# Retention attention into a snake feed-forward: the last nine chunks loaded head by head and worked in four 64x64 tiles

## The chip, the cores and the metric

The kernel runs on one core of a Trainium2 chip. The core has a matrix engine (TensorE: PE for its matmuls, PEld for its weight loads), three elementwise engines (VectorE = DVE, ScalarE = ACT, GpSimd = POOL) and SyncE (SP), which here only issues transfers. The transfers run on 16 DMA engines that all queues share. The metric is the device time of one execution in microseconds (us), as a median of several runs. A profile is one further execution that the hardware recorded; its span is the time from the first to the last instruction.

## What is computed

```python
# q, k, v: (4, 8, 768, 64) float32; gamma[h] = 1 - 2**(-5 - h), scale = 1/8
for t in range(S):
    state = gamma * state + k[:, :, t] (outer) v[:, :, t]
    y[:, :, t] = scale * q[:, :, t] @ state
x = y.transpose(0, 2, 1, 3).reshape(3072, 512)
h = x @ w_in                        # (512, 2048)
g = h + sin(alpha * h)**2 / (alpha + 1e-9)
out = g @ w_out                     # (2048, 512) -> (3072, 512) float32
```

## The kernel before

**Tiling.** Each of the 4 batches is cut into 6 chunks of 128 tokens, so there are 24 chunks. A chunk is worked for its 8 heads together. `P` is the order in which the chunks are worked: `P[0..3]` are the first chunks of the four batches (`e0` to `e3`), then come chunks 1 to 5 of batch 0 (`P[4..8]`), of batch 1 (`P[9..13]`), of batch 2 (`P[14..18]`) and of batch 3 (`P[19..23]`). The nine chunks that the change touches are `P[15..18]` and `P[19..23]`.

**Attention of a chunk.** `turn` (L202) has the DMA engines transpose q and k of the chunk into `qkT`, issued on SP. `stage_A` (L207) makes the scores of all 8 heads with 8 matmuls (L213), each with 64 rows and 128 columns of the array, and VectorE multiplies them by a causal mask into `aT` (L217). `stage_M` (L236) adds two products in `py`: the state times q (8 matmuls, L247) and `aT` times v (8 matmuls, L251), both in 128 rows and 64 columns. VectorE takes `py` out times the q decay into `xT` (L258). `stage_S` (L220, 8 matmuls, L227) adds k times v to the state `ps`, which stays in PSUM for a batch, and `keep_S` (L231) copies it to the block-diagonal `s_bd` on ScalarE. The decay of v is multiplied into v beforehand by `scale_v` (L111), from `P[6]` on on GpSimd.

**Feed-forward.** The chunks are taken in seven groups of 4, 2, 4, 4, 4, 4 and 2 chunks (`sizes`, L49). `phase` (L392) does the first product of a group in 16 slots (8 for the two groups of two): a `Slot` is 4 matmuls with `w_in` (L279), Sin and Square on ScalarE, and one combining instruction on VectorE (L294). In the same slot stand matmuls with `w_out` of the group before (`ff_out`, L304). So the PE always has a slot of 4 + 4 matmuls of 128x512. I write (g, n) for slot n of group g.

**Where attention stands.** The attention of a group's chunks is set into the slots of the group before: `where` (L538) puts `P[11..14]` at slots 5, 8, 11 and 14 of group 2, `P[15..18]` at slots 2, 6, 10 and 14 of group 3, `P[19..22]` at the same slots of group 4, and `P[23]` at (5,6). At `where[n]` stand, in this order, the scores of `P[n]`, the rest of `P[n-1]`, and the transpose of `P[n+2]` (L552 to L560). Everything on an engine runs in the order in which the program writes it (`manual_schedule`).

**Loads.** All chunk loads are issued by GpSimd, q, k and v of a chunk each in one transfer that also turns float32 to bf16 (`load_chunk`, L73; L83). GpSimd's program alternates three loads and a decay of v (L504 to L517); a load also waits in the program for the load eight before it, whose semaphore it takes over. The list runs down to `P[23]`, and the decays of `e2` and `e3` stand behind the loads of `P[13]` and `P[15]`.

Of the kernel before, what the change touches and what calls it, by code (L numbers as in the profile page):

```python
# [8 lines left out]
F32 = mybir.dt.float32  # L9
BF16 = mybir.dt.bfloat16  # L10
ACTF = mybir.ActivationFunctionType
ALU = mybir.AluOpType
# [3 lines left out]
def kernel(  # L16
# [15 lines left out]
    nc = tc.nc  # L32
    B, H, S, D = q.shape
    C = 128
    NCH = S // C
    NJ = B * NCH
    NP = H // 2
    d_model = H * D
    d_ff = moe_w_in.shape[1]
    KS = d_model // 128  # L40
# [8 lines left out]
    sizes = [4, 2, 4, 4, 4, 4, 2]  # L49
# [3 lines left out]
    place = {j: (g, i) for g, js in enumerate(groups) for i, j in enumerate(js)}  # L53

    consts = ctx.enter_context(tc.tile_pool(name="consts", bufs=1))
    big = ctx.enter_context(tc.tile_pool(name="big", bufs=1))
    work = ctx.enter_context(tc.tile_pool(name="work", bufs=2))
    psum = ctx.enter_context(tc.tile_pool(name="psum", bufs=1, space=bass.MemoryType.PSUM))
# [8 lines left out]
    raw = {}  # L67

    def chunk_of(t, j):
        b, c = divmod(j, NCH)  # L70
        return t[b, :, c * C:(c + 1) * C, :].rearrange("h s d -> s h d")

    def load_chunk(j, names="qkv"):  # L73
        for name, src in (("q", q), ("k", k), ("v", v)):
            if name not in names:
                continue
            if name == "v":
                t = big.tile([128, H, D], BF16, name="vr", tag="vr", bufs=NJ)
            else:
                if ("qk", j) not in raw:  # L80
                    raw["qk", j] = big.tile([128, 2, H, D], BF16, name="qkr", tag="qkr", bufs=NJ)
                t = raw["qk", j][:, "qk".index(name)]
            nc.gpsimd.dma_start(out=t, in_=chunk_of(src, j))  # L83
            raw[name, j] = t

    WP = 4
    fw = d_ff // WP
# [8 lines left out]

    near = {}
    for name, src in (("q", q), ("k", k)):
        near[name] = big.tile([128, H, D], F32, name=f"{name}0")
        nc.sync.dma_start(out=near[name], in_=chunk_of(src, 0))  # L100
        raw[name, 0] = big.tile([128, H, D], BF16, name=f"{name}b")
    alpha_row = consts.tile([FF, 128], F32, name="alpha_row")
# [2 lines left out]
    tio = consts.tile([128, C], F32, name="tio")  # L105
    nc.gpsimd.iota(tio, pattern=[[1, C]], channel_multiplier=0, base=0, allow_small_or_imprecise_dtypes=True)
    pos = consts.tile([128, NCH], F32, name="pos")
# [1 line left out]


    def scale_v(j, eng):  # L111
        eng.tensor_mul(raw["v", j], raw["v", j], kg[:, j % NCH, :, None].to_broadcast([128, H, D]))  # L112

    load_chunk(0, "v")
    load_chunk(order[1])
# [20 lines left out]
    lg = consts.tile([128, H], F32, name="lg")  # L136
# [14 lines left out]
    for p in range(NP):  # L151
        for e in range(2):
# [2 lines left out]
    expo = consts.tile([128, NCH, H], F32, name="expo")  # L155
    nc.vector.tensor_mul(expo, pos[:, :, None].to_broadcast([128, NCH, H]),
                         lg[:, None, :].to_broadcast([128, NCH, H]))
    qg = consts.tile([128, NCH, NP, C], F32, name="qg")
    kg = consts.tile([128, NCH, H], F32, name="kg")
    step = consts.tile([128, NCH, NP], F32, name="step")  # L160
# [8 lines left out]
    alpha_sb = consts.tile([128, FF], F32, name="alpha_sb")  # L169
    rec_alpha = consts.tile([128, FF], F32, name="rec_alpha")  # L170
    s_bd = [big.tile([128, NP, 128], BF16, name=f"s_bd{i}") for i in range(2)]


    st = {}
    xT = {}

    def half_T(j, i, eng):

        if i == 0:
            st["qkT", j] = work.tile([128, 2 * NP, 128], BF16, name="qkT", tag="qkT", bufs=6)  # L180
        pt = psum.tile([128, NP, 128], BF16, name="pt", tag="mm", bufs=4)
        for p in range(NP):
            nc.tensor.transpose(pt[:, p, :], raw["qk"[i], j][:, 2 * p:2 * p + 2, :].rearrange("p h d -> p (h d)"), ident)
        o = st["qkT", j][:, i * NP:(i + 1) * NP, :]
        if eng is nc.scalar:
            nc.scalar.copy(o, pt)
        else:
            nc.vector.tensor_copy(o, pt)
# [13 lines left out]
    def turn(j):  # L202

        st["qkT", j] = work.tile([128, 2 * NP, 128], BF16, name="qkT", tag="qkT", bufs=6)
        nc.sync.dma_start_transpose(out=st["qkT", j], in_=raw["qk", j].rearrange("p i h d -> p (i h d)"))

    def stage_A(j):  # L207
        qkT = st["qkT", j]
# [22 lines left out]
    def keep_S(j, ps):  # L231
        for e in range(2):
            r = slice(64 * e, 64 * e + 64)
            nc.scalar.copy(s_bd[(j % NCH + 1) % 2][r, :, r], ps[r, :, :])  # L234

    def stage_M(j):  # L236
        c = j % NCH
        g, i = place[j]
        if g not in xT:
            xT[g] = work.tile([128, KS, sizes[g] * C], BF16, name="xT", tag="xT", bufs=3)  # L240
        qkT, aT, vs = st["qkT", j], st["aT", j], raw["v", j]
        py = psum.tile([128, NP, 128], F32, name="py", tag="ty")
        if c > 0:
            for p in range(NP):
                for e in range(2):
                    r = slice(64 * e, 64 * e + 64)
                    nc.tensor.matmul(py[r, p, :], s_bd[c % 2][:, p, r], qkT[:, p, :],  # L247
                                     start=(p == 0), stop=True, skip_group_check=True)
        for p in range(NP):
            for e in range(2):  # L250
                nc.tensor.matmul(py[64 * e:64 * e + 64, p, :], vs[:, 2 * p + e, :], aT[:, e, p, :],  # L251
                                 start=(c == 0 and p == 0), stop=True, skip_group_check=True)
        x = xT[g][:, :, i * C:(i + 1) * C]
        if c == 0:
            nc.scalar.copy(x, py)
            return
        ps = stage_S(j) if c < NCH - 1 else None
        nc.vector.tensor_mul(x, py, qg[:, c])  # L258
        if ps is not None:
            keep_S(j, ps)  # L260


    gT = {}
# [72 lines left out]
    def out_pieces(g, tss):  # L336
        return [lambda ts=ts, f=f: ff_out(g, ts, f) for ts in tss for f in range(FF)]
# [5 lines left out]
    def idle_work(n):  # L343
        for _ in range(n):
            nc.tensor.matmul(spare["ps"], warm[:, :128], warm, start=True, stop=True)  # L345
# [5 lines left out]
    e0, e1, e2, e3 = order[:B]  # L351
# [4 lines left out]
    idle_work(2)  # L356
    nc.vector.tensor_mul(dec.rearrange("p e n t -> p (e n) t"), dec.rearrange("p e n t -> p (e n) t"), mask_bc)
    half_T(e0, 1, nc.scalar)
    nc.scalar.activation(out=kg, in_=expo, func=ACTF.Exp, scale=-1.0)
    for c in range(1, NCH):  # L360
        nc.scalar.activation(out=step[:, c, :], in_=lgp, func=ACTF.Exp, scale=float(C * c))
    idle_work(2)
    stage_A(e0)
    half_T(e1, 0, nc.scalar)
# [20 lines left out]
    decay_table(1)  # L385
    idle_work(5)
    stage_M(e2)
    decay_table(2)
    idle_work(3)


    def phase(g, outs, att, nf=1):  # L392

        no, done = len(outs), 0
        for n in range(FF // nf):
            now = Slot(g, n * nf, nf=nf).sq("A")
            for fn in att.get(n, ()):
                fn()
            now.add()
            while done < no * (n + 1) * nf // FF:  # L400
                outs[done]()
                done += 1
# [4 lines left out]
    def X(j):  # L407
        return lambda: turn(j)

    def A(j):  # L410
        return lambda: stage_A(j)

    def M(j):
        return lambda: stage_M(j)

    def SK(j):
        return lambda: keep_S(j, stage_S(j))
# [3 lines left out]
    P = order  # L421
    n3, n4 = 3 * C, 4 * C
    def F(ts, fs):
        for f in fs:
            for t in ts:
                ff_out(0, t, f)

    def early(f, tag="mm"):
        return Slot(0, f, (0, n3), tag=tag)

    a = early(0)
# [4 lines left out]
    b = early(1)  # L436
    a.sq("A").add()
    a = early(2)
    b.sq("A")
    c = early(3)  # L440
# [3 lines left out]
    b = early(4, "ps")  # L444
    c.sq("A")
    a.add()
    a = early(5)
# [3 lines left out]
    c = early(6)  # L451
    a.sq("A")
    b.add()
    b = early(7)
# [7 lines left out]
    F((0,), range(4))  # L462
    F((1,), range(3))
    b.add()
    a = Slot(0, 0, (n3, n4), 4)
    F((1,), (3,))
    a.sq("A").add()
    a = Slot(0, 8)
    b = Slot(0, 4, (n3, n4), 4)
    a.sq("A").add()  # L470
    a = Slot(0, 9)
    b.sq("D").add()
    F((0, 1), (4,))
    b = Slot(0, 10)
    a.sq("A").add()
    F((0, 1), (5,))
    a = Slot(0, 11)
# [3 lines left out]
    b = Slot(0, 12)  # L481
# [3 lines left out]
    a = Slot(0, 13)  # L485
    b.sq("D").add()
    F((0, 1), (9,))
    b = Slot(0, 14)
# [3 lines left out]
    a = Slot(0, 15)  # L492
# [16 lines left out]
    load_chunk(P[10])  # L509
    scale_v(P[8], nc.gpsimd)  # L510
    scale_v(e1, nc.gpsimd)
    for n in range(11, NJ + 2):
        scale_v(P[n - 2], nc.gpsimd)
        if n < NJ:
            load_chunk(P[n])
        if n in (13, 15):
            scale_v(P[(n - 9) // 2], nc.gpsimd)  # L517

    outs = out_pieces(0, (2, 3))

# [17 lines left out]
    where = {10: (2, 1)}  # L538
    for g in range(2, NG - 1):
        first = P.index(groups[g + 1][0])  # L540
# [8 lines left out]
    def at(place, fn):  # L549
        atts[place[0]].setdefault(place[1], []).append(fn)  # L550

    for n in range(10, NJ + 1):  # L552
        if n < NJ:
            at(where[n], A(P[n]))
        if n > 10:
            at(where[n], M(P[n - 1]))
        if n < NJ and P[n] % NCH == 1:
            at(where[n], SK(P[n] - 1))
        if n + 2 < NJ:
            at(where[n], X(P[n + 2]))  # L560
    for g in range(2, NG):
        phase(g, out_pieces(g - 1, range(sizes[g - 1])), atts[g], 1 if sizes[g] > 2 else 2)
    for fn in out_pieces(NG - 1, range(sizes[-1] - 1)):
# [30 lines left out]
```

## Time and profile before

| What | Value |
|---|---|
| Time of the kernel, 4 runs | median 216.48 us (216.33 to 218.24) |
| Profiled execution: its own time / its span | 216.54 us / 214.8 us |
| PE busy share; POOL, DVE, ACT | 96%; 42%, 59%, 76% |
| Mean granted TensorE clock | 1.000 |
| A decay of v on POOL (L112), x21 | 1058 ns each |
| `aT` on DVE (L217, 128x1024), x20 | 1220 ns each |
| `xT` on DVE (L258, 128x512), x20 | 682 ns each |
| Copy of the state on ACT (L234, 64x256), x40 | 360 ns each |

The profile's page gives for each group of instructions the busy time, the mean of one and the idle time of the engine before it with what ended it. A matmul's duration there includes its way through the array; what one costs in a row of many is the distance between the starts of neighbours. The "chain that ended last" is followed back from the last instruction, at each step to what released it.

### The profile page before, as it was taken

What the parts mean: (1) busy time and instruction counts of PE and PEld (TensorE: products, weight loads), DVE (VectorE), ACT (ScalarE), POOL (GpSimd) and SP (SyncE); (2) the same over time, 40 slices, a digit from 0 to 9 for tenths busy, and PEclk for the clock granted to TensorE, in tenths of its full rate; (3) what the DMA queues carried; (4) which work ended last, traced back from release to release, by engine and by line L of the source; (5) the groups of instructions that cost most, each with busy time, mean ns of one, the idle gap of its engine ahead of it and who ended that gap; (6) DMA issues with size and microseconds to landing.
All of it is one profiled execution on the core that took longest, in us unless ns stands there. A gap on an engine that the chain in (4) does not pass through costs nothing.

```text
span 214.8 us, 4304 instructions
## 1 busy us (share of the span) xinstructions
PE 206.1 (96%) x1685; PEld 108.7 (51%) x1685; DVE 127.5 (59%) x213; ACT 162.6 (76%) x311; POOL 90.0 (42%) x105
## 2 busy tenths in 40 slices
PE   7898899999999999999999999999999999999994
PEld 3444554466764545544544554554444444566554
DVE  4785669866896777774664664664644545333311
ACT  7778796658889898897787787787778877666630
POOL 8976335998669699695992300000000000000000
PEclk9999999999999999999999999999999999999999
DMA  9999999999999999999999743041011001111112
GB/s 130 149 196 187 205 207 169 154 139 240 147 150 202 147 156 153 153 159 184 130 154 143 90 101 89 9 102 50 2 49 52 32 16 49 52 49 49 52 49 98
DMA packets 100852, 24.93 MB, mean 116 GB/s; under 512 B 93392, under 2 KB 97888, under 8 KB 100832
## 3 DMA queue, kind: packets, MB, share of 16 engines
q0 software_dynamic: 77024, 13.37, 84.4%
q1 hardware_dynamic: 23808, 11.28, 26.7%
q8 instruction: 13, 0.21, 0.4%
q14 instruction: 7, 0.06, 0.1%
HBM read 27.27 MB, written 6.29 MB: 156 GB/s over the span
## 4 chain that ended last, share of the span: by engine, by line
PE 76%; DVE 10%; DMA 4%; POOL 4%; ACT 3%; issue 1%; POOLq 0%; DVEq 0%
PE po L304 35%; PE ph L279 31%; DVE gT L294 5%; DMA qkr<-in_k_dram 4%; PE py L247 3%; PE pa L213 2%; POOL qkr L83 2%; DVE aT L217 2%; PE py L251 2%; PE poh L327 2%; ACT s L282 2%; POOL vr L83 1%; ACT s L287 1%; PE ps L227 1%; DVE xT L258 1%
## 5 line engine op out<-in xcount | busy, mean ns | idle before, releaser
L294 DVE SCALAR_TENSOR_TENSOR gT<-s,rec_alpha,ph 128x512 bf16<-128x512 f32 (+3 forms) x120 | 74.1, 637 | 70.9 <-ACT s L287 70.5
L279 PE MATMUL ph<-xT,w_in 128*128 128x512 bf16 (+3 forms) x480 | 98.0, 336 | 0.8 <-DVE gT L294 0.5
L304 PE MATMUL po<-w_out,gT 128*128 128x512 bf16 x368 | 95.0, 380 | 0.6 <-DVE gT L294 0.6
L282 ACT ACTIVATE s<-ph,alpha_sb 128x512 f32<-128x512 f32 (+3 forms) x120 | 69.6, 601 | 33.1 <-PE ph L279 33.0
L279 PEld LDWEIGHTS <-w_in 128*128 128x128 bf16 x480 | 45.5, 98 | 42.3 <-issue 1.4
L287 ACT ACTIVATE s<-s 128x512 f32<-128x512 f32 (+1 forms) x94 | 58.4, 621 | 2.6
L304 PEld LDWEIGHTS <-gT 128*128 128x128 bf16 x368 | 33.9, 98 | 36.7 <-issue 0.6
L112 POOL TENSOR_TENSOR vr<-vr,kg 128x512 bf16<-128x512 bf16 x21 | 22.0, 1058 | 17.4 <-DMA vr<-in_v_dram 17.4
L217 DVE TENSOR_TENSOR aT<-pa,mask 128x1024 bf16<-128x1024 f32 x20 | 24.4, 1220 | 0.3 <-PE pa L213 0.3
L83 POOL DMA_DIRECT2D vr<-in_v_dram x24 | 21.8, 907 | 3.3 <-DMA w_in<-in_moe_w_in_dram 1.7
L83 POOL DMA_DIRECT2D qkr<-in_q_dram x23 | 21.3, 927 | 4.1 <-DMA w_out<-in_moe_w_out_dram 1.7
L83 POOL DMA_DIRECT2D qkr<-in_k_dram x23 | 20.5, 891 | 3.7 <-DMA w_out<-in_moe_w_out_dram 3.3
L234 ACT CAST s_bd<-ps 64x256 bf16<-64x256 f32 x40 | 14.4, 360 | 2.4 <-PE ps L227 2.1
L316 ACT COPY o_sb<-po 128x512 f32<-128x512 f32 x23 | 13.1, 576 | 3.9 <-PE po L304 3.9
L258 DVE TENSOR_TENSOR xT<-py,qg 128x512 bf16<-128x512 f32 x20 | 13.6, 682 | 1.1 <-PE py L251 1.1
L345 PE MATMUL spare<-warm 128*128 128x512 bf16 x28 | 9.3, 456 | 1.2 <-DVE warm L131 1.2
L213 PEld LDWEIGHTS <-qkT 64*128 64x128 bf16 x192 | 5.4, 94 | 10.0 <-issue 6.7
L213 PE MATMUL pa<-qkT 64*128 64x128 bf16 x192 | 9.5, 219 | 0.9 <-DMA qkT<-qkr 0.3
L251 PE MATMUL py<-aT,vr 128*64 128x128 bf16 x192 | 9.5, 220 | 0.4 <-DVE rec_alpha L383 0.2
L247 PE MATMUL py<-qkT,s_bd 128*64 128x128 bf16 x160 | 8.3, 225 | 0.1
L251 PEld LDWEIGHTS <-vr 128*64 128x64 bf16 x192 | 6.8, 110 | 1.3 <-issue 1.0
L247 PEld LDWEIGHTS <-s_bd 128*64 128x64 bf16 x160 | 5.2, 109 | 3.3 <-ACT s_bd L234 0.8
(61 smaller groups left out, 74.1 us busy)
## 6 DMA issues: line engine op xcount, KB each, us to landing
out_dram<-o_sb SPq DMA_DIRECT2D x23, 256.0 KB, 2.3
vr<-in_v_dram POOLq DMA_DIRECT2D x24, 128.0 KB, 6.7
qkr<-in_q_dram POOLq DMA_DIRECT2D x23, 128.0 KB, 5.8
qkr<-in_k_dram POOLq DMA_DIRECT2D x23, 128.0 KB, 5.9
w_in<-in_moe_w_in_dram POOLq DMA_DIRECT2D x4, 512.0 KB, 10.7
w_out<-in_moe_w_out_dram POOLq DMA_DIRECT2D x4, 512.0 KB, 14.6
qkT<-qkr SPq DMA_TRANSPOSE x17, 6.3
q<-in_q_dram SPq DMA_DIRECT2D x1, 256.0 KB, 3.2
```

Of the source, the lines that this page charges most:

```text
L83: nc.gpsimd.dma_start(out=t, in_=chunk_of(src, j))
L112: eng.tensor_mul(raw["v", j], raw["v", j], kg[:, j % NCH, :, None].to_broadcast([128, H, D]))
L213: nc.tensor.matmul(pa[:, e, p, :], qkT[r, NP + p, :], qkT[r, p, :], start=(p == 0), stop=True, skip_group_check=True)
L217: nc.vector.tensor_mul(aT.rearrange("p e n t -> p (e n) t"), pa.rearrange("p e n t -> p (e n) t"), m)
L247: nc.tensor.matmul(py[r, p, :], s_bd[c % 2][:, p, r], qkT[:, p, :], start=(p == 0), stop=True, skip_group_check=True)
L251: nc.tensor.matmul(py[64 * e:64 * e + 64, p, :], vs[:, 2 * p + e, :], aT[:, e, p, :], start=(c == 0 and p == 0), stop=True, skip_group_che ...
L258: nc.vector.tensor_mul(x, py, qg[:, c])
L279: nc.tensor.matmul(self.ph[:, m, :], w_in[:, i, f * 128:(f + 1) * 128], xT[g][:, i, self.lo:self.hi], start=(m == 0 and i == 0), stop=(i = ...
L282: nc.scalar.activation(out=self.s[:, m, :], in_=self.ph[:, m, :], func=ACTF.Sin, scale=alpha_sb[:, f:f + 1])
L287: nc.scalar.activation(out=self.s, in_=self.s, func=ACTF.Square)
L294: nc.vector.scalar_tensor_tensor(gT[self.g][:, f, self.lo:self.hi], self.s[:, m, :], rec_alpha[:, f:f + 1], self.ph[:, m, :], op0=ALU.mult ...
L304: nc.tensor.matmul(po[g, ts], gT[g][:, f, ts * C:(ts + 1) * C], w_out[:, f, :], start=(f == 0), stop=(f == FF - 1))
```

## The change

`wide(j)` is true for the nine chunks. They are loaded by `load_seq`, batch by batch: q, then k, then v, and of each one transfer per head, 64 partitions wide: heads 0 to 3 on partitions 0 to 63, heads 4 to 7 on 64 to 127, so that a chunk is two half chunks of 64 tokens side by side. That is 48 transfers where 27 were. On GpSimd, decays of v stand between these rows of 8 transfers, and those of `P[19..23]` stand behind all loads, at `where[n]`.

For these chunks the attention becomes one `burst` of matmuls: `inter` (state times q) in 4 matmuls of the full array, then the scores of the new chunk, the product with v of the old one and its new state in 64x64 tiles, four of which cover the array. The state is no longer kept in PSUM but added in SBUF in `s_f` by VectorE (`keep`), and `hand` copies it to `s_bd`, on ScalarE in batch 2 and on GpSimd in batch 3. The exit, `keep` and `hand` run one slot after the burst. The scores have 768 columns in place of 1024, since the later half's keys need no scores with the earlier half's queries. Small tables for the new layout are made at the start (`later_tables`, `later_mask`).

```diff
+    def wide(j):
+        return j >= 2 * NCH + 2 and j != 3 * NCH
+
+    def load_seq(bt, names="qkv"):
+
...
+        tqk, tv = raw["seq", bt]
+        for name, src in (("q", q), ("k", k), ("v", v)):
+            if name not in names:
+                continue
+            for h in range(H):
+                r = slice(64 * (h // NP), 64 * (h // NP) + 64)
+                o = tv[r, :, h % NP, :] if name == "v" else tqk[r, :, "qk".index(name), h % NP, :]
+                nc.gpsimd.dma_start(out=o, in_=src[bt, h, cs[0] * C:, :].rearrange("(f i) d -> i f d", i=64))
+        for i, c in enumerate(cs):
+            j, f = bt * NCH + c, slice(2 * i, 2 * i + 2)
+            raw["qk", j], raw["k", j], raw["v", j] = tqk[:, f], tqk[:, f, 1], tv[:, f]
...
-        near[name] = big.tile([128, H, D], F32, name=f"{name}0")
+        near[name] = work.tile([128, d_model], F32, name="o_sb", tag="o_sb", bufs=3).rearrange("i (h d) -> i h d", h=H)
...
-        eng.tensor_mul(raw["v", j], raw["v", j], kg[:, j % NCH, :, None].to_broadcast([128, H, D]))
+        t, by = raw["v", j], kg
+        if wide(j):
+            t, by = t.rearrange("i f p d -> i (f p) d"), kgq
+        eng.tensor_mul(t, t, by[:, j % NCH, :, None].to_broadcast([128, H, D]))
...
+    def later_tables():
+        for b in range(2):
+            r = slice(64 * b, 64 * b + 64)
+            for f in range(2):
+                nc.vector.tensor_scalar_add(tok[r, :, f], pos[r, :], float(64 * (f - b)))
+            nc.vector.tensor_copy(lgq[r], lg[r, NP * b:NP * b + NP])
+        for f in range(2):
+            nc.vector.tensor_mul(expoq[:, :, NP * f:NP * f + NP],
+                                 tok[:, :, f, None].to_broadcast([128, NCH, NP]),
+                                 lgq[:, None, :].to_broadcast([128, NCH, NP]))
+
+    def later_mask():
+        for b in range(2):
+            nc.vector.tensor_scalar(maskq[64 * b:64 * b + 64, 0:128], tio[64 * b:64 * b + 64],
+                                    tok[64 * b:64 * b + 64, 0, 0:1], None, op0=ALU.is_ge)
+        nc.vector.tensor_copy(maskq[:, 128:192], maskq[:, 0:64])
...
+    tiles4 = [(b, e) for b in range(2) for e in range(2)]
+    def inter(j):
+        qkT, s = st["qkT", j], s_bd[j % NCH % 2]
+        st["py", j] = [psum.tile([128, 512], F32, name=f"py{b}", tag=tag) for b, tag in enumerate(("ps", "ty"))]
+        for m in range(2):
+            for b in range(2):
+                nc.tensor.matmul(st["py", j][b][:, m * 128:(m + 1) * 128].rearrange("p (f i) -> p f i", f=2),
+                                 s[:, 2 * b + m, :], qkT[:, m:m + 5:4, half(b)],
+                                 start=(m == 0), stop=True, skip_group_check=True)
+    def scores(j):
+        qkT = st["qkT", j]
+        pa = psum.tile([128, 2, 512], F32, name="pa", tag="pa")
+        for m in range(2):
+            for b, e in tiles4:
+                nc.tensor.matmul(pa[half(b), e, 192 * m:192 * m + 128].rearrange("p (f i) -> p f i", f=2),
+                                 qkT[half(e), 2 + m, half(b)], qkT[half(e), m:m + 5:4, half(b)],
+                                 start=(m == 0), stop=True, skip_group_check=True)
+            for b, e in tiles4:
+                nc.tensor.matmul(pa[half(b), e, 192 * m + 128:192 * m + 192],
+                                 qkT[half(e), 6 + m, half(b)], qkT[half(e), 4 + m, half(b)],
+                                 start=False, stop=True, skip_group_check=True)
+        aT = work.tile([128, 2, 2, 192], BF16, name="aTw", tag="aT", bufs=2)
+        st["aT", j] = aT
+        return {"mask": lambda: nc.vector.tensor_mul(aT, pa[:, :, 0:384].rearrange("p e (m t) -> p e m t", m=2),
+                                                     maskq[:, None, None, :].to_broadcast([128, 2, 2, 192]))}
+    def mix(j, first=None):
+        py, aT, vs, c = st["py", j], st["aT", j], raw["v", j], j % NCH
+        for m in range(2):
+            for b, e in tiles4:
+                nc.tensor.matmul(py[b][half(e), m * 128:(m + 1) * 128], vs[half(b), 0, 2 * m + e, :],
+                                 aT[half(b), e, m, 0:128], start=False, stop=True, skip_group_check=True)
+            for b, e in tiles4:
+                nc.tensor.matmul(py[b][half(e), m * 128 + 64:(m + 1) * 128], vs[half(b), 1, 2 * m + e, :],
+                                 aT[half(b), e, m, 128:192], start=False, stop=True, skip_group_check=True)
+        now = j if c < NCH - 1 else first
+        if now is not None:
+            ks, vs = raw["k", now], raw["v", now]
+            for f in range(2 if wide(now) else 1):
+                for m in range(2):
+                    for b, e in tiles4:
+                        h = 4 * b + 2 * m + e
+                        nc.tensor.matmul(py[b][half(e), 256 + 64 * m:320 + 64 * m],
+                                         ks[half(b), f, 2 * m + e, :] if wide(now) else ks[:, h, :],
+                                         vs[half(b), f, 2 * m + e, :] if wide(now) else vs[:, h, :],
+                                         start=False, stop=True, skip_group_check=True)
...
+        def leave():
+            for b in range(2):
+                nc.vector.tensor_mul(x[:, 2 * b:2 * b + 2, :], py[b][:, 0:256].rearrange("p (m t) -> p m t", m=2),
+                                     qg[:, c, 2 * b:2 * b + 2])
+        def keep():
+            for b in range(2):
+                o, new = s_f[:, 2 * b:2 * b + 2], py[b][:, 256:384].rearrange("p (m d) -> p m d", m=2)
+                if wide(now):
+                    nc.vector.tensor_add(o, o, new)
+                else:
+                    nc.vector.tensor_copy(o, new)
+        def hand():
+            for e in range(2):
+                copy = nc.scalar.copy if now // NCH == 2 else nc.gpsimd.tensor_copy
+                copy(s_bd[(now % NCH + 1) % 2][half(e), :, half(e)], s_f[half(e)])
+        more = {"exit": leave}
+        if now is not None:
+            more.update(keep=keep, hand=hand)
+        return more
+    def burst(old, new, first=None):
+        inter(old)
+        return {**(scores(new) if new is not None else {}), **mix(old, first)}
...
             now = Slot(g, n * nf, nf=nf).sq("A")
+            run(more, "keep", "exit", "hand")
             for fn in att.get(n, ()):
-                fn()
+                fresh.update(fn() or {})
+            run(fresh, "mask")
+            if fresh:
+                rest[0] = fresh
             now.add()
...
-    for n in range(11, NJ + 2):
+    for n in range(11, 15):
         scale_v(P[n - 2], nc.gpsimd)
-        if n < NJ:
-            load_chunk(P[n])
-        if n in (13, 15):
-            scale_v(P[(n - 9) // 2], nc.gpsimd)
+        load_chunk(P[n])
+    load_seq(2, "q")
+    scale_v(P[13], nc.gpsimd)
+    scale_v(e2, nc.gpsimd)
+    load_seq(2, "k")
+    scale_v(P[14], nc.gpsimd)
+    load_seq(2, "v")
+    scale_v(e3, nc.gpsimd)
+    load_seq(3, "q")
+    scale_v(P[15], nc.gpsimd)
+    scale_v(P[16], nc.gpsimd)
+    load_seq(3, "k")
+    scale_v(P[17], nc.gpsimd)
+    scale_v(P[18], nc.gpsimd)
+    load_seq(3, "v")
...
+    def M_last(j):
+        stage_M(j)
+        nc.vector.tensor_copy(s_f, st["ps"])
+    def B(old, new, first):
+        return lambda: burst(old, new, first)
     for n in range(10, NJ + 1):
-        if n < NJ:
-            at(where[n], A(P[n]))
-        if n > 10:
-            at(where[n], M(P[n - 1]))
-        if n < NJ and P[n] % NCH == 1:
-            at(where[n], SK(P[n] - 1))
+        new = P[n] if n < NJ else None
+        first = new - 1 if n < NJ and new % NCH == 1 else None
+        if n > 10 and wide(P[n - 1]):
+            at(where[n], B(P[n - 1], new, first))
+        else:
+            at(where[n], lambda j=new: (scores if wide(j) else stage_A)(j))
+            if n > 10:
+                at(where[n], lambda j=P[n - 1], last=wide(new): (M_last if last else stage_M)(j))
+            if first is not None:
+                at(where[n], SK(first))
         if n + 2 < NJ:
             at(where[n], X(P[n + 2]))
+        if n >= 19 and n < NJ:
+            at(where[n], lambda j=new: scale_v(j, nc.gpsimd))
```

More of the change, by code (lines that the diff above doesn't have):

```diff
@@ L77, in load_chunk @@
             if name == "v":
-                t = big.tile([128, H, D], BF16, name="vr", tag="vr", bufs=NJ)
+                t = big.tile([128, H, D], BF16, name="vr", tag="vr", bufs=NJ - 9)
             else:
                 if ("qk", j) not in raw:
-                    raw["qk", j] = big.tile([128, 2, H, D], BF16, name="qkr", tag="qkr", bufs=NJ)
+                    raw["qk", j] = big.tile([128, 2, H, D], BF16, name="qkr", tag="qkr", bufs=NJ - 10)
                 t = raw["qk", j][:, "qk".index(name)]
@@ L84, in load_chunk @@
             raw[name, j] = t
+    def wide(j):
+        return j >= 2 * NCH + 2 and j != 3 * NCH
+    def load_seq(bt, names="qkv"):
+        cs = [c for c in range(NCH) if wide(bt * NCH + c)]
+        nh = 2 * len(cs)
+        if "q" in names:
+            raw["seq", bt] = (big.tile([128, nh, 2, NP, D], BF16, name=f"qk_seq{bt}"),
+                              big.tile([128, nh, NP, D], BF16, name=f"v_seq{bt}"))
+        tqk, tv = raw["seq", bt]
[9 more added lines that the diff above has]
+            raw["qk", j], raw["k", j], raw["v", j] = tqk[:, f], tqk[:, f, 1], tv[:, f]
     WP = 4
@@ L157 @@
                          lg[:, None, :].to_broadcast([128, NCH, H]))
+    kgq = consts.tile([128, NCH, H], F32, name="kgq")
+    expoq = consts.tile([128, NCH, H], F32, name="expoq")
+    tok = consts.tile([128, NCH, 2], F32, name="tok")
+    lgq = consts.tile([128, NP], F32, name="lgq")
+    maskq = consts.tile([128, 192], BF16, name="maskq")
+    def later_tables():
[13 more added lines that the diff above has]
+        nc.vector.tensor_copy(maskq[:, 128:192], maskq[:, 0:64])
     qg = consts.tile([128, NCH, NP, C], F32, name="qg")
@@ L171 @@
     s_bd = [big.tile([128, NP, 128], BF16, name=f"s_bd{i}") for i in range(2)]
+    s_f = big.tile([128, NP, D], F32, name="s_f")
     st = {}
@@ L204, in turn @@
         st["qkT", j] = work.tile([128, 2 * NP, 128], BF16, name="qkT", tag="qkT", bufs=6)
-        nc.sync.dma_start_transpose(out=st["qkT", j], in_=raw["qk", j].rearrange("p i h d -> p (i h d)"))
+        nc.sync.dma_start_transpose(out=st["qkT", j], in_=raw["qk", j].rearrange(
+            "i a f p d -> i (a f p d)" if wide(j) else "i a h d -> i (a h d)"))
     def stage_A(j):
@@ L260, in stage_M, with half @@
             keep_S(j, ps)
+    def half(x):
+        return slice(64 * x, 64 * x + 64)
+    tiles4 = [(b, e) for b in range(2) for e in range(2)]
[7 more added lines that the diff above has]
+                                 start=(m == 0), stop=True, skip_group_check=True)
@@ new lines, in mix @@
+    def mix(j, first=None):
[18 more added lines that the diff above has]
+                                         start=False, stop=True, skip_group_check=True)
+        g, i = place[j]
+        if g not in xT:
+            xT[g] = work.tile([128, KS, sizes[g] * C], BF16, name="xT", tag="xT", bufs=3)
+        x = xT[g][:, :, i * C:(i + 1) * C]
+        def leave():
[17 more added lines that the diff above has]
+        return more
@@ L263, with run @@
+    def burst(old, new, first=None):
+        inter(old)
+        return {**(scores(new) if new is not None else {}), **mix(old, first)}
+    def run(more, *kinds):
+        for kind in kinds:
+            if more and kind in more:
+                more.pop(kind)()
     gT = {}
@@ L358 @@
     half_T(e0, 1, nc.scalar)
+    later_tables()
     nc.scalar.activation(out=kg, in_=expo, func=ACTF.Exp, scale=-1.0)
@@ L361 @@
         nc.scalar.activation(out=step[:, c, :], in_=lgp, func=ACTF.Exp, scale=float(C * c))
+    nc.scalar.activation(out=kgq, in_=expoq, func=ACTF.Exp, scale=-1.0)
     idle_work(2)
@@ L389 @@
     idle_work(3)
+    rest = [{}]
     def phase(g, outs, att, nf=1):
@@ L395, in phase @@
         for n in range(FF // nf):
+            more, fresh = rest[0], {}
             now = Slot(g, n * nf, nf=nf).sq("A")
+            run(more, "keep", "exit", "hand")
             for fn in att.get(n, ()):
-                fn()
+                fresh.update(fn() or {})
+            run(fresh, "mask")
+            if fresh:
+                rest[0] = fresh
             now.add()
@@ L464 @@
     b.add()
+    later_mask()
     a = Slot(0, 0, (n3, n4), 4)
```

## The prediction, made before the changed kernel ran

> **What bounds the kernel now.** I read the waits first. From 66 us to 210 us no line of them has a matmul of PE waiting for another engine, and the weight loads' only entries of size are "issue", time in which nothing is waited for:
>
> ```profile
> engine line waited for: us in total, times, longest us
> DVE gT L294 <- ACT s L287: 61.9, 57, 1.7
> ACT s L282 <- PE ph L279: 25.2, 46, 1.1
> POOL vr L112 <- DMA vr<-in_v_dram: 12.9, 7, 4.1
> PEld L213 <- issue: 5.9, 14, 0.4
> ```
>
> So in the stretch that the change rewrites, each engine waits in the end for PE, and a saved PE microsecond is a saved microsecond. The chain of waits in order of time shows what attention takes of it; columns are start, length, what:
>
> ```profile
> 101.78 0.86 PE ph L279 x4
> 102.65 0.33 PE pa L213 x8
> 102.98 0.34 PE py L247 x8
> 103.32 0.22 PE py L251 x8
> 103.54 0.12 PE ps L227 x8
> 103.67 0.97 PE po L304 x4
> 104.64 0.86 PE ph L279 x4
> ```
>
> A slot is 0.86 + 0.86. Around attention the next po piece takes 0.97, so a chunk costs 0.33+0.34+0.22+0.12+0.11 = 1.12 us. Last the loads, since the change moves them. The GpSimd timeline up to the load of P[15] (at 75.73) and of P[16]:
>
> ```profile
> 70.16 0.94 POOL L83 DMA_DIRECT2D qkr<-in_q_dram  x1
> 71.09 0.88 POOL L83 DMA_DIRECT2D qkr<-in_k_dram  x1
> 71.96 0.89 POOL L83 DMA_DIRECT2D vr<-in_v_dram  x1
> 74.74 1.04 POOL L112 TENSOR_TENSOR vr<-vr,kg 128x512 bf16<-128x512 bf16 x1 [1.89 <-DMA vr<-in_v_dram]
> 75.73 0.95 POOL L83 DMA_DIRECT2D qkr<-in_q_dram  x1
> 76.67 0.89 POOL L83 DMA_DIRECT2D qkr<-in_k_dram  x1
> ```
>
> In the trace, k of P[15] landed at 81.8, SP issued its transpose at 81.9, that landed at 89.1, and its scores start at 94.55 (slot (3,2)). The margin is 5.5 us: small for a change that asks for four chunks' q and k first.
>
> **PE: what a burst costs.** In the single instructions at 142.4 to 143.8, two partner tiles start 3 ns apart and the pairs follow each other every 55 ns with 128 columns of data, every 30 ns with 64. Each change of tile shape leaves a hole: 312 ns instead of 216 from L279 to L213 (96), 144 instead of 55 to L247 (89, then 25 on its first pair), 128 instead of 30 to L304 (98, then 10). Sum for before: 96+11+4x55+89+25+8x55+4x30+98+10 = 1.11.
>
> No row shows four tiles at once. One bound: all four run like a pair does (55 and 30 ns a set). The other: two at a time (110 and 60). I take the first, since the pairs show both splits, rows (L213) and columns (L247), each wholly concurrent. Then: inter 4x55 = 220 in the shape of its neighbours, no hole; hole 110; scores 2x(55+30) = 170; mix 170; state 4x30 = 120; hole 108. Sum 0.90, so 0.22 less.
>
> By stage: P[16..18], P[20..23] are seven such bursts, 7 x 0.22 = 1.5. At P[15] (old-form rest, new-form scores) 0.05; at P[19] (the state of e3 has 128-row tiles, one more hole) 0.1; the last rest alone 0.05. **PE saves 1.7 us.**
>
> The Trainium skill speaks against this: "TensorEngine Tiling (Array Packing)", Performance Considerations, Instruction Overhead, gives each matmul some 60 cycles whatever its width. Were that paid one after another, at half of the 55 ns that 128 columns take, the 48 small matmuls of a burst would cost 48 x 27 = 1.3 us, and a burst 1.3+0.22+0.22 = 1.74, or 0.6 more than before: nine of them +5.6. The row of L227 weighs more: 8 matmuls with 64 columns in 0.12, 15 ns each, because partners share the time. I keep -1.7.
>
> **DVE, ACT.** The mask is 128x768: between 0.68 (512) and 1.22 (1024) that is 0.95. The two exits at 128x256 come to 0.41 each, the two keeps at 128x128 to 0.28. In a burst slot DVE has 0.95+0.75, in the next 0.56+0.82+0.75. They stand before the next L294, which waits about 1 us for ACT in every slot (the first line of waits), and that wait hides them. The tight place is a group's last exit: P[17] and P[21] leave in slot 15, and the next group's first L279 reads them. From the timeline at 142: burst at 142.65, mask 143.4 to 144.3, L294 to 145.0, keeps to 145.5, exits at 145.9 and 146.25; the slot after ends at 146.15, and its third matmul is the first to need the second exit (146.6). I put **0.1** for both; if the cover is gone, an exit, 0.4 each. hand replaces the copies of L234: two of 0.36 on ACT as before, on POOL in batch 3 at up to 1.06 each (its decay row), with 7 us until the next inter. keep, exit and hand free the PSUM banks three slots before the next burst.
>
> **Start.** later_tables puts eight small DVE instructions (0.06 to 0.21 each by rows L153 and L156, 1.0 together) before aT of e0, where DVE idles 0.56; kgq adds 0.25 on ACT. Up to 0.5 late on PE, but the early slots then wait for loads (PE idle 0.65 at 17.6 until q of e3 lands): nothing, or 0.5 without that wait. later_mask (0.5 twice, plus a copy of 0.1) stands before the L294 at 27.91, where DVE idles 2.57: nothing, or 1.1 without that gap. q0 and k0 in o_sb are read out by 6 us, the first store is at 44: nothing.
>
> **Loads.** POOL's price of a load: rows of 1024 pieces are 0.865 apart, those of w_in and w_out with 512 pieces 0.735 (7.63 to 9.10, two). So 64x8x64 (512 pieces) is 0.735, 64x10x64 is 0.765. POOL is free for load_seq after P[14]'s loads, 1 us earlier than before as e2 has moved: 71.9. q of batch 2: 8 x 0.735 = 5.9, 77.8. Decays of P[13] and e2: 2.0, 79.8. k: 5.9, 85.7. P[15]'s transpose needs all sixteen. DMA keeps up: three loads of 1024 pieces land about 0.9 apart where no transpose runs beside them (89.6, 90.6, 91.6), so 0.45 for half a load.
>
> Landing: the DMA skill page ("DMA: Bandwidth & Descriptors", Anatomy of one DMA) prices a transfer of GpSimd at about 2 us fixed plus bytes, so 2.2 here; the fastest chunk loads in the trace took 3.6, the median 5.9. With 3.6 after the last issue (84.9), k is there at 88.5; by the rule 87.1. The transpose takes 6.3 (median row; 4.8 to 7.4 beside loads): 94.8, plus 0.3 of semaphores and SP, 95.1. **Stall at P[15]: 0.6 us**; by the rule none. The bounds are 0 (POOL cheaper with 64 partitions) and 5 (below). SP queues behind this transpose only P[16]'s, due at 102.6, and the store at 91.75, which goes out 2 us before o_sb is needed: nothing.
>
> Behind it: P[14]'s decay at 86.7 (needed 94.9), v to 92.6, e3 to 93.6 (needed 126), q of batch 3 to 99.7, P[15]'s decay to 100.8 (needed 103), P[16]'s 101.8, k to 108, P[17] and P[18] to 110, v to 116. P[19]'s transpose waits on SP from 107.9 to about 112 with one store behind it that is due at 115; its scores are due at 126.7. P[19..23]'s decays have 8 us each.
>
> **Sum.** -1.7 + 0.1 + 0.6 = -1.0 against the profiled execution's 216.54 (214.8 span and 1.7 around it, 0.06 over the median 216.48): **215.5 us**.
>
> **Rivals.** *Loads late (slower).* The place is the scores of P[15], which PE cannot pass. If a half load costs POOL as much as a whole one, 16 x 0.865 = 13.8, and k is issued at 87.8; if it lands after 5, 92.8, and the transpose takes 7, 99.8: stall 5.2, total 216.5-1.7+0.1+5.2 = 220.1. It decides the sign once that transpose lands after 96.2, and passes 1% after 98.3. For it: nearly double the transfers, 16 needed before the first chunk. Against: the row of 512 pieces.
> *Two tiles at a time.* Burst 220+110+340+340+240+108 = 1.36, 0.24 more; with the smaller stages +2.2: 219.4 with the same stall. Then the change does not do what it says. Against: both splits run concurrently alone.
> *No stall, tighter sets.* 53 and 27 ns, holes 90: 0.28 saved a burst, 2.3 in all: 214.3.
>
> **How the numbers follow.** About 1% is what a measurement of this kernel can tell from no change: 214.3 and 218.6. Forecast (four tiles, stall 0 to 2): 0.62, 214.8 to 216.9. Loads late: 0.18, two thirds of it over 218.6. Two tiles or in part: 0.13, nearly all over. No stall and tighter: 0.07, which with the forecast's lower edge gives faster 0.08; slower 0.24; same 0.68. Range 214.5 to 218.9: it leaves out the last case and the far half of the slow ones.
>
> **What would show it.** In the single matmuls four starts within some 12 ns, sets 55 and 30 ns apart, a burst of 0.90 in the chain; if sets are 110, the second rival. At (3,2) a wait of PE for DMA qkT of 0 to 2 us; POOL's seq loads 0.735 apart. An L279 waiting for DVE xT at the start of groups 4 and 5 of over 0.2, or a burst waiting for POOL's v, would be a price that I left out.

## The result and the profile after

The changed kernel takes 215.66 us (median of 43 runs) where the kernel before, run beside it, takes 217.09 (64 runs): ratio 0.9932, 95% interval 0.9919 to 0.9945, so 1.5 us less. Forecast was 1.0 less. (The four earlier runs of the kernel before, from which the forecast started, had a median of 216.48.) The profiled execution has a span of 213.2 us after 214.8.

The page of the changed kernel, section 4, the chain by engine:

```profile
PE 80%; DVE 11%; ACT 5%; issue 2%; DVEq 0%; ACTq 0%
```

PE bounds it as before, when its share of the chain was 76%. The waits of PE's weight loads from 66 to 210 us (engine, line, what it waited for, us in total, times, longest) are these two lines, and for matmuls there is none:

```profile
PEld L265 <- issue: 2.1, 5, 0.4
PEld L337 <- issue: 0.4, 1, 0.4
```

No stall at P[15]: its scores (L337) waited for no other engine and no transfer; the same 0.4 of "issue" stands before each set of scores of the older form (L265). The chain in order of time shows a burst. L327 is the state times q, L337 and L341 are the scores, L354 and L357 the product with v, L366 the new state; L425 and L450 are the feed-forward's L279 and L304 of before. Columns are start, length, what:

```profile
110.41 0.22 PE py L327 x4
110.63 0.18 PE pa L337 x4
110.81 0.03 PE pa L341 x4
110.84 0.06 PE pa L337 x4
110.90 0.03 PE pa L341 x4
110.93 0.06 PE py L354 x4
110.99 0.03 PE py L357 x4
111.02 0.06 PE py L354 x4
111.08 0.03 PE py L357 x4
111.11 0.13 PE py L366 x16
111.23 0.97 PE po L450 x4
```

Four matmuls of 128 columns go by in 0.06, four of 64 in 0.03, and the 16 of the state in 0.13. From 110.41 to 111.23 plus the 0.11 that po is longer makes 0.93; before it was 1.12. The best measure is the distance from the scores of one chunk to those of the next, four slots and one attention: 8.03 us before, 7.83 after, the same in every full burst. In the timelines, before and after:

```profile
142.75 0.40 PE L213 MATMUL pa<-qkT 64*128 64x128 bf16 x8
150.78 0.40 PE L213 MATMUL pa<-qkT 64*128 64x128 bf16 x8
142.02 0.25 PE L337 MATMUL pa<-qkT 64*64 64x128 bf16 x4
149.85 0.25 PE L337 MATMUL pa<-qkT 64*64 64x128 bf16 x4
```

From P[15]'s scores to the end of the span it is 120.22 before and 118.69 after. These 1.53 us are the whole difference in the spans (1.57), and the runs show 1.5.

GpSimd's timeline of the loads of batch 2 (start, length, what, idle time before it):

```profile
70.99 2.77 POOL L103 DMA_DIRECT2D qk_seq<-in_q_dram  x4
74.33 0.68 POOL L103 DMA_DIRECT2D qk_seq<-in_q_dram  x1 [0.56 <-DMA vr<-in_v_dram]
75.62 0.68 POOL L103 DMA_DIRECT2D qk_seq<-in_q_dram  x1 [0.61 <-DMA qkr<-in_q_dram]
76.52 0.68 POOL L103 DMA_DIRECT2D qk_seq<-in_q_dram  x1 [0.22 <-DMA qkr<-in_k_dram]
78.00 0.68 POOL L103 DMA_DIRECT2D qk_seq<-in_q_dram  x1 [0.81 <-DMA vr<-in_v_dram]
78.70 2.05 POOL L137 TENSOR_TENSOR vr<-vr,kg 128x512 bf16<-128x512 bf16 x2
80.69 5.48 POOL L103 DMA_DIRECT2D qk_seq<-in_k_dram  x8
```

The waits in brackets are for the load eight before. k is issued by 86.2 and its last piece landed at 88.1; the transpose of P[15] was issued at 88.3 and landed at 92.9; the scores start at 94.5. So 1.7 us of the former 5.5 us of margin are left.

### The profile page after: what moved, and what is told of

Its sections match the earlier page's. It is cut to its first block, busy times and chain, and to the rows that moved or that the text cites. A ratio compares the mean times of both kernels' runs of the same rounds, so it can differ in the third digit from the quotient of the medians.

```text
span 213.2 us, 4694 instructions
## 1 busy us (share of the span) xinstructions
PE 204.6 (96%) x1849; PEld 109.2 (51%) x1849; DVE 132.0 (62%) x250; ACT 159.9 (75%) x302; POOL 103.4 (49%) x136
## 4 chain that ended last, share of the span: by engine, by line
PE 80%; DVE 11%; ACT 5%; issue 2%; DVEq 0%; ACTq 0%
PE po L450 34%; PE ph L425 32%; DVE gT L440 4%; PE spare L491 3%; ACT s L428 3%; DVE aT L269 2%; PE poh L473 2%; PE pa L265 1%; PE py L299 1%; PE py L303 1%; ACT s L433 1%; PE pa L337 1%; PE py L327 1%; DVE xT L310 1%; DVE s L435 1%
## 5 line engine op out<-in xcount | busy, mean ns | idle before, releaser
L425 PE MATMUL ph<-xT,w_in 128*128 128x512 bf16 (+3 forms) x480 | 98.0, 336 | 0.6 <-DVE gT L440 0.5
L450 PE MATMUL po<-w_out,gT 128*128 128x512 bf16 x368 | 95.2, 380 | 0.7 <-DVE gT L440 0.6
L425 PEld LDWEIGHTS <-w_in 128*128 128x128 bf16 x480 | 45.5, 98 | 42.1 <-issue 1.8
L450 PEld LDWEIGHTS <-gT 128*128 128x128 bf16 x368 | 33.9, 98 | 37.0 <-issue 1.0
L83 POOL DMA_DIRECT2D vr<-in_v_dram x15 | 13.7, 916 | 3.2 <-DMA w_in<-in_moe_w_in_dram 1.7
L83 POOL DMA_DIRECT2D qkr<-in_q_dram x14 | 12.8, 916 | 4.2 <-DMA w_in<-in_moe_w_in_dram 1.7
L137 POOL TENSOR_TENSOR vr<-vr,kg 128x512 bf16<-128x512 bf16 x12 | 12.7, 1072 | 3.8 <-DMA vr<-in_v_dram 3.3
L83 POOL DMA_DIRECT2D qkr<-in_k_dram x14 | 12.5, 896 | 3.7 <-DMA w_out<-in_moe_w_out_dram 3.3
L269 DVE TENSOR_TENSOR aT<-pa,mask 128x1024 bf16<-128x1024 f32 x11 | 13.4, 1217 | 0.3 <-PE pa L265 0.3
L103 POOL DMA_DIRECT2D qk_seq<-in_q_dram x16 | 11.3, 760 | 2.2 <-DMA vr<-in_v_dram 1.4
L103 POOL DMA_DIRECT2D v_seq<-in_v_dram x16 | 11.4, 803 | 0.0
L137 POOL TENSOR_TENSOR v_seq<-v_seq,kgq 128x512 bf16<-128x512 bf16 x9 | 9.6, 1109 | 3.5 <-DMA v_seq<-in_v_dram 3.2
L103 POOL DMA_DIRECT2D qk_seq<-in_k_dram x16 | 11.3, 777 | 0.0
L346 DVE TENSOR_TENSOR aTw<-pa,maskq 128x768 bf16<-128x768 f32 x9 | 8.6, 954 | 0.7
```

What stands on the lines that cost most here:

```text
L103: nc.gpsimd.dma_start(out=o, in_=src[bt, h, cs[0] * C:, :].rearrange("(f i) d -> i f d", i=64))
L137: eng.tensor_mul(t, t, by[:, j % NCH, :, None].to_broadcast([128, H, D]))
L269: nc.vector.tensor_mul(aT.rearrange("p e n t -> p (e n) t"), pa.rearrange("p e n t -> p (e n) t"), m)
L425: nc.tensor.matmul(self.ph[:, m, :], w_in[:, i, f * 128:(f + 1) * 128], xT[g][:, i, self.lo:self.hi], start=(m == 0 and i == 0), stop=(i = ...
L450: nc.tensor.matmul(po[g, ts], gT[g][:, f, ts * C:(ts + 1) * C], w_out[:, f, :], start=(f == 0), stop=(f == FF - 1))
```

## The experiments

All are edits of the changed kernel, whose lines they move by a few. Of each I give the ratio to the kernel before, and the distance between scores (full bursts: 8.03 before, 7.83 in the changed kernel), which is free of what happens in the start.

**Two tiles at a time, and one at a time.** The loops over tiles stand outside those over the sets (the same edit in the scores, the product with v and the state):

```diff
-        for m in range(2):
-            for b, e in tiles4:
+        for some in (tiles4[0::3], tiles4[1:3]):      # one at a time: [[t] for t in tiles4]
+            for m in range(2):
+                for b, e in some:
```

> The small matmuls of a burst are written two tiles at a time (diagonal tiles first, then the other two), all else as in the changed kernel. My theory, that the gain comes from four tiles sharing the time: sets of 110 and 60 ns, scores 170 to 340, product with v 170 to 340, state 120 to 240, so a burst takes 1.36 in place of 0.92 us; over the nine places +3.9 us on the changed kernel, about 219.5, slower than before by 1.1%. Rival, that the gain comes from the dropped shape change, the shorter scores and the state in SBUF, and the order of the tiles means nothing: within 0.3 us of the changed kernel.

> The small matmuls are written tile by tile: all of one tile, then all of the next. Theory: matmuls start in the program's order, so only the last of a tile overlaps the first of the next. Scores 4 x 170 less 3 overlaps of 30 = 590, product with v 590, state 16 x 30 less 3 x 30 = 390 ns; burst 0.92 + 0.42 + 0.42 + 0.27 = 2.03, about +1.1 at each of seven bursts and +0.4 to +0.7 at the other places: +9 us, about 224.5. Rival as for the pairs: no change; a second rival, that instructions cost the same in any order: no change.

Two at a time: ratio 0.9958 (0.9934 to 0.9981), distance 7.88. One at a time: 0.9976 (0.9953 to 0.9999), distance 7.93. My expectation fell: +0.05 and +0.10 a burst, not +0.44 and +1.1. The chain of the run with one tile at a time:

```profile
111.53 0.20 PE pa L338 x4
111.73 0.03 PE pa L342 x2
111.76 0.06 PE pa L338 x4
111.81 0.03 PE pa L342 x2
```

The program has all of the first tile's scores before the second tile's, yet the four tiles' first 128-column matmuls still stand together. In the single instructions they start at 111.459, .472, .486 and .499, and the first tile's second matmul, which is before three of these in the program, starts only at 111.539. A tile's matmuls wait for one another, not for those of other tiles. The 13 ns between two tiles fit the four matmuls of a tile at the 3.3 ns that lie between neighbours' starts in the changed kernel (110.565, .568, .571, .575), and where two tiles are written at a time, with eight matmuls ahead of the other two, it is 26 (112.034 to 112.060). I read this as matmuls that are handed out in the program's order every 3.3 ns and then wait only within their own tile. So the order could not break the concurrency, and the runs did not tell my theory from its rival.

**The concurrency measured.** Each 128-column matmul of the scores and of the product with v is done twice, the second time into unread PSUM columns, in all tiles or in the first alone. In the scores (the product with v likewise):

```diff
+            for b, e in tiles4:                       # or tiles4[:1]
+                nc.tensor.matmul(pa[half(b), e, 384:512].rearrange("p (f i) -> p f i", f=2),
+                                 qkT[half(e), 2 + m, half(b)], qkT[half(e), m:m + 5:4, half(b)],
+                                 start=False, stop=True, skip_group_check=True)
```

> Each matmul with 128 columns in the scores and in the product with v is done a second time, into columns of PSUM that nobody reads: 16 matmuls more in a full burst, 4 in each tile. Theory, four tiles share the time: each tile's stream grows by 4 x 55 = 0.22 us, and so does the burst; with half of it at P[15] and at the last, from slot (3,0) to the end 123.1 + 2.0 = 125.1. Rival, two share it: 0.44, 127.1. Rival, one after another: 0.88, 131.

> The same second matmuls, but for the first of the four tiles alone: 4 more in a full burst. Theory, independent streams, the longest sets the burst: also +0.22 a burst, 125.1 from slot (3,0) to the end. Rival, that the matmuls cost by their number: a quarter of what doubling all costs, +0.5, 123.6.

All tiles: distance 8.06, 125.10 from slot (3,0) to the end, ratio 1.0019 (0.9995 to 1.0044). One tile: 8.05, 125.02, ratio 1.0010 (0.9976 to 1.0043). Sixteen more matmuls cost what four cost, 0.22 and 0.21 us: four tiles share the time wholly, and the longest stream sets the burst. The timelines, two lines with all tiles doubled, then four with one:

```profile
119.94 0.25 PE L337 MATMUL pa<-qkT 64*64 64x128 bf16 x4
128.00 0.25 PE L337 MATMUL pa<-qkT 64*64 64x128 bf16 x4
119.20 0.25 PE L337 MATMUL pa<-qkT 64*64 64x128 bf16 x4
119.28 0.22 PE L341 MATMUL pa<-qkT 64*64 64x128 bf16 x1
119.29 0.20 PE L345 MATMUL pa<-qkT 64*64 64x64 bf16 x3
127.25 0.25 PE L337 MATMUL pa<-qkT 64*64 64x128 bf16 x4
```

While the first tile does its second copy (L341), the other three go on with their next matmul (L345). The rivals of two at a time and of cost by number are refuted.

**What the gain is made of.** First, the state times q in 64-column tiles as before the change:

```diff
-                nc.tensor.matmul(st["py", j][b][:, m * 128:(m + 1) * 128].rearrange("p (f i) -> p f i", f=2),
-                                 s[:, 2 * b + m, :], qkT[:, m:m + 5:4, half(b)],
+                for e in range(2):
+                    nc.tensor.matmul(st["py", j][b][half(e), m * 128:(m + 1) * 128].rearrange("p (f i) -> p f i", f=2),
+                                     s[:, 2 * b + m, half(e)], qkT[:, m:m + 5:4, half(b)],
```

> The state times q is done in 8 matmuls of 128 rows and 64 columns as before the change, not in 4 of the full array. Theory: pairs at 55 ns give the same 220 ns, but one more change of shape in each burst, 89 + 25 ns by the profile of before: +0.11 a burst, +1.0 us over nine, about 216.6, so that the gain on before falls from 1.5 to about 0.5 us. Rival, that only the tiles count: no change against the changed kernel.

Distance 7.96, so +0.12; ratio 1.0003 (0.9973 to 1.0034). The chain shows where:

```profile
112.05 0.34 PE py L328 x8
```

The state times q takes 0.34 in place of 0.22, all of it the additional change of shape with its slow first pair. Then the quarter of the scores and of the product with v that the half chunks leave out is done all the same (into unread columns), in the changed kernel and in the one just shown:

```diff
+            for b, e in tiles4:
+                nc.tensor.matmul(pa[half(b), e, 384 + 64 * m:448 + 64 * m],
+                                 qkT[half(e), 6 + m, half(b)], qkT[half(e), m, half(b)],
+                                 start=False, stop=True, skip_group_check=True)
```

> The quarter of the work that the half chunks leave out (the later half's keys with the earlier half's queries, and v of the later half with it) is done all the same, into PSUM columns that nobody reads: 4 more sets of four 64-column matmuls in a full burst. Theory, that the burst's gain of 0.20 us is 0.11 from one change of shape less plus 0.11 from this quarter, and nothing from four tiles as against two: +4 x 28 ns = 0.11 a burst, from slot (3,0) to the end 123.1 + 0.9 = 124.0, against 124.6 before. Rival, that four tiles are faster in themselves: the same here, but see the next run.

> The quarter done and the state times q in 64-column tiles, so that burst and old attention have the same work and the same number of shape changes; only the four tiles are left of the change to PE. Theory: 123.1 + 0.9 + 1.07 = 125.1 from slot (3,0) to the end, the whole gain gone, at most 0.5 slower than before (124.6). Rival, that four tiles are faster in themselves: clearly under 124.6, by the part that they bring.

With the quarter: distance 7.96, so +0.13; ratio 1.0001 (0.9979 to 1.0024). With both: distance 8.08, against 8.03 before the change; ratio 1.0099 (1.0065 to 1.0133). So of the 0.20 us, the dropped change of shape is 0.12 and the left-out quarter 0.13; with neither, four tiles are 0.05 slower than the two tiles of twice the size that ran at a time before. Four at once are thus no gain by themselves here. What the tiles bring is that scores, product with v and state fit into one shape, and that a quarter can be left out. By the ratios the last run is 3.6 us above the changed kernel, while the two edits alone add 1.07 and 1.15 from slot (3,0) to the end of their profiles, so some 1.4 are left over. Its profile ran 1.5 us longer behind the last chunk's scores than that of the first edit alone, and DVE waited there 1.9 us for a store. That part is open.

**The margin of the loads.** First, k of batch 2 ahead of the two decays:

```diff
     load_seq(2, "q")
+    load_seq(2, "k")
     scale_v(P[13], nc.gpsimd)
     scale_v(e2, nc.gpsimd)
-    load_seq(2, "k")
```

> The two decays of v between q and k of batch 2 stand behind k. Theory: k of batch 2 is issued 2 us earlier and P[15]'s transpose lands at about 91, but its scores start at 94.6 as in the changed kernel since PE comes there no sooner: same time within 0.2 us. Rival, that the loads still cost something there or elsewhere: faster by up to 0.6 us (the stall that I had put into the sum).

Ratio 0.9927 (0.9899 to 0.9954), distance 7.83, no wait at P[15]: the same time. But k, issued by 84.9 in place of 86.2, landed at 89.1 in place of 88.1, in a profile in which q had landed 0.8 later too: it was not GpSimd alone that set its landing. Then idle decays ahead of k, two or five:

```diff
     scale_v(e2, nc.gpsimd)
+    idle = big.tile([128, H, D], BF16, name="idle")
+    nc.gpsimd.memset(idle, 0.0)
+    for _ in range(5):                                # or 2
+        nc.gpsimd.tensor_mul(idle, idle, kg[:, 0, :, None].to_broadcast([128, H, D]))
     load_seq(2, "k")
```

> Two idle decays (2.1 us on GpSimd, on a tile of their own) stand before the loads of k of batch 2. Theory, that the loads are covered by a margin only: in the profiled runs so far P[15]'s transpose lands 0.3 to 1.7 us before its scores start, and scores start 4.41 us after slot (3,0) where nothing holds them. With 2.1 us of delay that distance becomes 4.8 to 6.2 and the time grows by 0.4 to 1.8 us on the changed kernel. Rival, that the DMA engines and not GpSimd set when k lands (k issued 1.2 us earlier landed no earlier in the run before): the distance stays 4.41 and the time the same.

> Five idle decays (5.3 us) at the same place. Theory: the stall at P[15]'s scores is 3.6 to 5.0 us, the distance from slot (3,0) 8.0 to 9.4, and the kernel slower than before by about 1.3 to 2% (my rival of loads that come late). Rival as for two: at most 2 us. The granted clock after the stall shows whether idle PE is paid for twice: theory 1.00, then the rest from (3,2) to the end is as long as in the changed kernel.

Two: ratio 1.0014 (0.9988 to 1.004). The waits of its weight loads show both places that I had named:

```profile
PEld L337 <- DMA qkT<-qk_seq: 1.4, 1, 1.4
PEld L354 <- POOL v_seq L137: 0.5, 1, 0.5
```

The scores of P[15] start 5.38 us after slot (3,0) in place of 4.41, and at (3,6) PE waits 0.5 for the decay of P[15]'s v, which all later loads stand behind. Five: ratio 1.0258 (1.0218 to 1.0298); the distance is 9.46, a stall of 5.0. From P[15]'s scores to the end it takes 121.2 us in place of 118.7, so the stall was paid for with 2.5 us more. The table by stretches shows where (length, busy us of PE, PEld, DVE, ACT and POOL, each with its number of instructions, then the granted clock, the busy share of the DMA engines and GB/s):

```profile
94.00:98.00 4.00, 0.79 (x4) 0.18 (x2) 0.75 (x1) 1.77 (x3) 4.00 (x7) 1.00 1.09 109
98.00:102.00 4.00, 1.90 (x41) 1.77 (x43) 0.67 (x1) 0.44 (x2) 4.00 (x7) 0.55 1.68 180
102.00:106.00 4.00, 4.00 (x12) 1.44 (x11) 1.97 (x4) 1.19 (x3) 3.61 (x6) 0.60 1.70 140
106.00:110.00 4.00, 4.00 (x21) 1.76 (x19) 1.50 (x2) 3.50 (x6) 3.99 (x5) 1.00 2.37 163
```

PE was idle from 94.8 to 99.8. The clock fell to one half at 98.4, 3.6 us after PE went idle, and came back at 105.2, 5.4 us after it began again. My expectation that the rest would take as long as before was wrong. After the 1.0 us stall with two decays it stayed at 1.00.

## Why the prediction was right, point by point

**The number.** The change was 1.5 us where I had 1.0. That the time itself, 215.5, was missed by only 0.2 is luck: PE saved 0.2 less than I had said, the 0.7 of stall and exits did not come, and the kernel before took 217.09 in 64 runs where four had 216.48.

**PE, -1.7: right, measured -1.5.** A burst saves 0.20, not 0.22. The sum was a little low: the change into 64x64 costs a hole of 95 ns (110.415 to 110.565, less 55) and 25 more on its first set (110.565 to 110.645, 80 in place of 55), 120 where I had put 110; and a state set takes 32 ns, not 30. My choice of bound, four at once, is shown by the doubled matmuls. The 60 cycles that the Trainium skill gives each matmul ("TensorEngine Tiling (Array Packing)", Instruction Overhead) do not add up over tiles: the 48 small ones of a burst took 0.47 us (110.565 to 111.040), against the 1.3 estimated from that page.

**Stall, +0.6: did not come.** The mis-sized term is the transpose's time to land: I took 6.3 us from the median of before, it was 4.6, and between 4.5 and 5.2 in all eleven profiles with the new loads. (Beside loads the trace of before has 4.8 to 8.5, not up to 7.4 as I read it.) It is now issued after only two or three half loads of v; that this is the reason is argued, not tested. In the same profile the next two transposes, with more loads issued by then, took 6.2 and 6.5, and the last three, with no load left, 3.1. The other terms of that sum missed in both directions: a half load costs GpSimd 0.68, not 0.735, but q waited 2.2 us for loads eight before, so k was issued at 86.2 (85.7 predicted). The last piece of k landed 2.7 us after its issue (85.4 to 88.1), between my 3.6 and the 2.2 estimated from the skill's rule ("DMA: Bandwidth & Descriptors", Anatomy of one DMA), and nearer the rule. Without the stall and the exit my sum is 214.8 in the terms of the profiled execution, 1.7 below; 1.5 was measured.

**Group ends, +0.1: nothing.** In DVE's timeline the second exit of P[17] runs to 121.74, and the next group's first L425 starts unhindered at 121.60; the margin is as small as worked out.

**Start, nothing: right in sum, wrong in its working.** The small tables take DVE 1.55 us and not 1.0 (7.15 to 8.70), aT of e0 starts 1.25 late and the first L425 at 15.98 in place of 14.86. The loads of e3 hid it: the L425 behind e3's transposes stands at 19.02 after 19.30 before, and slot (3,0) at 90.10 after 90.13. In the profiles of the experiments slot (3,0) starts anywhere from 90.3 to 91.6. Whether the tables have a part in that is open; a version with the tables earlier was not run. The ratio leaves room for little: it gives 1.5, within 0.3, and the part behind P[15]'s scores is 1.53.

**Rivals.** The loads that come late are real as a mechanism (two idle decays cost the whole gain) but lie 1.7 us beyond where the profile of the changed kernel stands, and in the seven experiments that leave the loads alone 0.2 to 1.6 us. The changed kernel thus stands near a stall. I priced them too low: 5 us of stall cost 7.6 in that span and 7.1 by the runs. Two tiles at a time is refuted. The third case, no stall, came true without its tighter sets.

## What to carry to other kernels

Where a bound engine does small work in several shapes, count the changes of shape first: here one more cost 0.12 us a burst, about what the left-out quarter of the scores and of the product with v costs (0.13). The four tiles paid here because they made one shape of several and let work be left out, not because there were more of them. When a change collects loads ahead of their first use, follow the last of them through issue, landing and what is issued on its landing, and look at the margin that stays, not only at whether there is a wait. Here a stall of 5.0 us on PE was paid for again with 2.5 us at a lower clock; one of 1.0 us was not.

## What was not expected of the hardware

Matmuls of different tiles overtake each other (the four tiles' first matmuls 13 ns apart although the program has three others of the first tile between them), so the order in which tiles are written costs 0.05 to 0.10 us a burst and not more. And after 5.0 us of idle time PE ran at half its clock for 5.4 us.
